# Second MLP, last block of 512 tokens: a seven-product contraction over two halves of 256 tokens, then the plain second contraction

## The chip, the cores and the metric

One NeuronCore of a Trainium2 chip runs the whole program in one launch. The metric is device time in microseconds (us). Engines are named as in the profile: PE (TensorE matmuls), PEld (TensorE weight loads, which overlap PE), DVE (VectorE), ACT (ScalarE), POOL (GpSimd) and SP (SyncE, which here only issues DMAs).

## What is computed

Attention without softmax and an RMS norm give 4608 tokens of 512 features. Two MLPs follow, each 512 -> 2048 -> 512, the first with a smooth clipped activation, the second with a squared ReLU. The change touches the second MLP alone:

```python
def _moe2_ref(x, w_in, w_out):       # x 4608 x 512, w_in 512 x 2048, w_out 2048 x 512
    h = x @ w_in
    r = np.maximum(h, 0.0)
    g = r * r
    return (g @ w_out).astype(np.float32)
```

All of it is asked for in float32. The kernel reaches that by splitting each operand into a high and a low part (type fp32r) and adding three matmuls for each product: high x high, high x low, low x high.

## The kernel before, in words

The 4608 tokens are handled as blocks of 512: eight blocks with the first 512 tokens of each batch, and a ninth (number 8) that collects the 64 remaining tokens of every batch. The first layer takes seven blocks one after the other (`h_stage`, `g_stage`, `out_stage`) while attention runs between them. After that, five steps each take two blocks at once, listed in `PAIRS` (line 130): (2,0), (2,2), (1, blocks 7 and 8), (2,4), (2,6), each entry the layer and its first block. Layer 2, block 8 is left, and is done at the end by plain contractions.

A step over two blocks uses a form of matrix multiplication with seven products of halves in place of eight. The halves are two of the tokens (the two blocks), two of the contracted dimension and two of the outputs. `in_phase(n)` (line 907) does the first contraction: 4 groups `q` of 7 `PRODUCTS` (order 1, 6, 2, 7, 5, 4, 3; line 70), for each product two output chunks `i`, and for each chunk two contracted chunks of three matmuls (`mm_group`, line 889), so 12 matmuls for one product. The seven products of a chunk gather in three PSUM banks (`bank_of`): the second product of a bank is added on top of what the first left there, after an engine has read it. ACT or DVE reads each bank after each product (lines 926 to 953) and makes the four quarters of the activated tile, `g2[k]`. `out_phase(n, jobs, at)` (line 964) does the second contraction in the same way, 56 steps, and its result stays in half of the `g2` tiles. During `out_phase(n)` the `jobs` prepare the tokens of the next step: `x2_jobs` (line 839) loads four chunks of the two blocks for each half of the features, and makes seven halved combinations `x2` of them.

The sums of halves of the weights were written to DRAM earlier (`wsd`). They come back as tiles of 512 KB, in exactly the order in which they are used (`w_order`, line 792). `take_w2` (line 816) hands over the next tile and issues, on SP, the load of the one seven places later; `w_ring` (line 783) has eight buffers, so that load waits until the matmuls on the tile before the present one are done.

The output of a step in layer 2 is written by four calls of `put_out` (line 1040). Each transposes two tiles on DVE and issues eight DMAs of 64 KB on SP, whose rows in DRAM are runs of 32 floats. The calls stand in the list `late` (line 1206) and are taken after products 0, 1, 5 and 9 of the next `in_phase` (line 1197), or after the first four steps of the last loop (line 1213). SP works through its queue in order: a weight load that stands behind eight of these DMAs is issued after them.

The last loop (lines 1208 to 1221) does block 8 of layer 2: 16 chunks `t` of the hidden dimension, each with 12 matmuls of the first contraction (`h_stage`, line 686, four feature chunks by three matmuls, 512 tokens wide), ACT and DVE for the activation and its two parts (`g_stage`, line 712), and, two steps behind (`LAG`), 12 matmuls of the second contraction with the activated tile as the stationary operand (`out_part`, line 718). One weight tile of each matrix is taken per chunk. `out_last` (line 746) finishes the last two chunks output by output and writes the results.

Of the kernel before, what the change touches and what calls it, by code (L numbers as in the profile page):

```python
# [9 lines left out]
F32 = mybir.dt.float32  # L10
# [66 lines left out]
def linear_attention_rms_two_mlps(  # L77
# [12 lines left out]
    nc = tc.nc  # L90
# [636 lines left out]
        mm3(acc[L, b][c], lhs, rhs, f == 0, f == NF - 1)  # L727

    def out_stage(L, b, f):
        if f == 0:  # L730
            acc[L, b] = [
                ps_a.tile([P, TB], F32, tag=f"acc{c}", name=f"acc{L}_{b}_{c}") for c in range(KD)
            ]
        for c in range(KD):
            out_part(L, b, f, c)
        del gs[L, b, f]
        if f == NF - 1:
            for c, a in enumerate(acc.pop((L, b))):
                t = st.tile([P, TB], F32, tag="st", name=f"ev{L}_{b}_{c}")
                if c % 2 == 0:  # L740
                    nc.vector.tensor_copy(t, a)
                else:
                    nc.scalar.copy(t, a)
                store(L, b, c, t)
# [48 lines left out]
    for L, _ in PAIRS:  # L793
        w_order += [(L, 0, q, p) for q in range(NQ) for p in PRODUCTS]
        w_order += [(L, 1, a, p) for p in PRODUCTS for a in range(NQ)]
    for f in range(NF + LAG):
        w_order += [(0, f)] * (f < NF) + [(1, f - LAG)] * (f >= LAG)
    w_loaded = []
    w_todo = iter(w_order)

# [15 lines left out]
    def take_w2(*key):  # L816


        found, t = w_loaded.pop(0)
        assert found == key, (found, key)  # L820
        load_w2()
        return t

    def halve(t, src, op):
        copy(engine2(op + "_hi"), t[:, 0, :], src)
        engine2(op + "_lo").tensor_tensor(t[:, 1, :], src, t[:, 0, :].bitcast(F32), ALU.subtract)  # L826

    x2 = {}

    def x_source(n, b, ch, t):  # L830

        L, b0 = PAIRS[n]
        if L == 2:
            return t, x1d[b0 + b][:, ch, :]
        if b == 0:
            return t, xpd[:, ch, :]
        return t.rearrange("p (b s) -> p b s", b=B), xrd[:, ch, :, :]

    def x2_jobs(n, ring):

        jobs = []
        for c in range(2):
            src = {}

            def load(c=c, src=src):
                for key, b, ch in ((11, 0, c), (12, 1, c), (22, 1, c + 2), (21, 0, c + 2)):
                    t = ring.tile([P, TB], F32, f"xr{n}_{c}_{key}")
                    nc.sync.dma_start(*x_source(n, b, ch, t))
                    src[key] = t

            def part(p, key, c=c, src=src, then=None):
                j = 7 * c + len([k for k in x2 if k[0] == n and k[2] == c])
                t = wp.tile([P, 2, TB], F32R, tag=f"w0_{j}", name=f"x2_{n}_{p}_{c}")
                halve(t, src[key], "x")
                x2[n, p, c] = t
                if then:
                    to, a, b = then
                    engine2("x_sum").tensor_tensor(src[to], src[a], src[b], ALU.subtract)  # L858

            jobs.append(load)  # L860

            for p, key, then in (
                (1, 11, (11, 12, 11)),
                (5, 11, (12, 22, 12)),
                (7, 12, (11, 22, 11)),
                (6, 11, None),
                (2, 21, (21, 21, 11)),
                (3, 22, None),
                (4, 21, None),
            ):  # L870
                jobs.append(lambda p=p, key=key, then=then, f=part: f(p, key, then=then))
        return jobs

    def x2_whole_jobs(L, b):
        src = {}

        def load(c):
            src[c] = tmp.tile([P, TB], F32, f"xr{b}_{c}")
            nc.sync.dma_start(src[c], x1d[b][:, c, :])

        def part(c):
            u = wp.tile([P, 2, TB], F32R, tag=f"w0_{c}", name=f"x2_{b}_{c}")
            halve(u, src[c], "x")
            xs.setdefault((L, b), []).append(u)

        order = ((load, 0), (load, 1), (part, 0), (load, 2), (part, 1), (load, 3), (part, 2), (part, 3))
        return [lambda f=f, c=c: f(c) for f, c in order]

    def mm_group(ps, lhs, rhs, first, last):

# [15 lines left out]

    def in_phase(n):

        for q in range(NQ):
            ps = {}  # L910
            e = {}
            for p in PRODUCTS:
                w = take_w2(PAIRS[n][0], 0, q, p)
                for i in range(2):
                    k = 2 * q + i
                    if p in FIRST:
                        ps[i, bank_of[p]] = ps_ring.tile([P, TB], F32, f"ph{n}_{p}_{k}")
                    bank = ps[i, bank_of[p]]
                    mm_group(
                        bank,  # L920
                        [lambda a, c=c: w[:, i, a, c * P : (c + 1) * P] for c in range(2)],
                        [lambda a, c=c: x2[n, p, c][:, a, :] for c in range(2)],
                        p in FIRST,
                        True,
                    )
                    if p == 1:
                        e[i, 1] = e_ring.tile([P, TB], F32, f"e1_{n}_{k}")
                        g2[k] = [
                            g_ring.tile([P, 2, TB], F32, f"g2_{n}_{k}_{j}") for j in range(2)
                        ]  # L930
                        nc.scalar.copy(e[i, 1], bank)
                    elif p in (6, 7):
                        kind = "e16" if p == 6 else "e167"
                        if p == 6:
                            e[i, 6] = e_ring.tile([P, TB], F32, f"{kind}_{n}_{k}")
                        else:
                            e[i, 7] = e_ring.tile([P, TB], F32, f"{kind}_{n}_{k}")
                        nc.vector.tensor_tensor(e[i, p], bank, e[i, 1], ALU.add)  # L938
                    else:
                        g = g2[k][0 if p in (2, 3) else 1][:, {2: 0, 3: 1, 4: 0, 5: 1}[p], :]  # L940
                        h = bank
                        if p != 2:
                            h = tmp.tile([P, TB], F32, f"h{n}_{p}_{k}")
                            add = e[i, {5: 7, 4: 1, 3: 6}[p]]
                            nc.vector.tensor_tensor(h, bank, add, ALU.add)  # L945
                        if PAIRS[n][0] == 1:
                            nc.scalar.activation(g, h, AF.Relu, bias=halfb, scale=0.5)
                            nc.scalar.activation(g, g, AF.Square)
                            nc.vector.scalar_tensor_tensor(g, g, 1.0, h, op0=ALU.min, op1=ALU.max)
                        else:  # L950
                            u = tmp.tile([P, TB], F32, f"u{n}_{p}_{k}") if p == 2 else h
                            nc.scalar.activation(u, h, AF.Relu)  # L952
                            nc.scalar.activation(g, u, AF.Square)  # L953
                yield
            for i in range(2):
                k = 2 * q + i
                a, b, d = g2[k][0][:, 0, :], g2[k][0][:, 1, :], g2[k][1][:, 1, :]
                t1[k] = t1_ring.tile([P, TB], F32, f"t1_{n}_{k}")
                engine2("t_sum").tensor_tensor(t1[k], b, a, ALU.subtract)
                engine2("t_sum").tensor_tensor(b, d, b, ALU.subtract)  # L960
# [227 lines left out]
        pay()  # L1188

    late = []  # L1190
    for n in range(NS):
        step_in = in_phase(n)
        for i, _ in enumerate(step_in):
            pay(True)
            if n == 0 and i < LAG:
                out_stage(*step(N1 - LAG + i))
            if late and i in (0, 1, 5, 9):
                late.pop(0)()
        while late:
            late.pop(0)()  # L1200
        result[n] = result_of(dict(g2))
        jobs = x2_jobs(n + 1, tmp) if n + 1 < NS else x2_whole_jobs(2, NB - 1)
        at = (2, *range(10, 8 + 2 * len(jobs), 2))
        for _ in out_phase(n, jobs, at):
            pass
        late = [lambda n=n, h=h: put_out(n, h // 2, h % 2) for h in range(4)]

    L, b = 2, NB - 1
    for t in range(NF + LAG):
        if t < NF:  # L1210
            wi[L, t] = take_w2(0, t)
            h_stage(L, b, t)
        if late:
            late.pop(0)()
        if t < NF:
            g_stage(L, b, t)
        if t >= LAG:
            wo[L, t - LAG] = take_w2(1, t - LAG)
        if LAG <= t < NF:
            out_stage(L, b, t - LAG)  # L1220
    out_last(L, b, *range(NF - LAG, NF))


# [34 lines left out]
```

## Time and profile before

| | us |
|---|---|
| median of 3 runs | 1565.77 (1565.66 to 1566.26) |
| the profiled execution: its own time | 1565.7 |
| its span, first to last instruction | 1563.9 |
| the two phases of the step before the last block | 1319.48 to 1395.64, and on to 1471.8 |
| last block, first to last matmul | 1471.8 to 1559.0 |

The page gives the busy time of each engine, the chain of work that ended last, and groups of instructions. A timeline lists instructions in order of time: when they began, how long the merged run of them lasted, engine, line, operation, what was written and read, shape and count; idle time of the engine just before stands in brackets with what ended it. The durations of single matmuls overlap each other, so the rate is read from the times at which runs begin. For a DMA the length is the time that SP spent on issuing it, and the landing is told apart.

### The profile page before, as it was taken

To read this page: it belongs to the slowest core of one execution; us is meant where nothing else is said; L and a number is where in the kernel's file an instruction comes from. 1 tells how busy PE (TensorE), PEld (TensorE's weight loads), DVE (VectorE), ACT (ScalarE), POOL (GpSimd) and SP (SyncE) were. 2 spreads that over 40 slices of the span, in tenths; PEclk is the share of its full clock that TensorE was granted. 3 is DMA by queue.
4 is the path that set the end of the run, shared out by engine and by line. 5 is a ranking of instruction groups with operands and counts; after the bars stand their busy time and mean duration, and the time that the engine had idled before them with its cause. 6 is when DMAs were issued, how large, how long until landed. Compare 5 with 4: busy or idle time off the path is not lost.

```text
span 1563.9 us, 21429 instructions
## 1 busy us (share of the span) xinstructions
PE 1553.6 (99%) x7437; PEld 1275.3 (82%) x7437; DVE 1097.4 (70%) x1871; ACT 940.1 (60%) x1719; POOL 17.3 (1%) x38
## 2 busy tenths in 40 slices
PE   9999999999999999999999999999999999999998
PEld 5788888888888888888888888888888888888887
DVE  6976786877877786754597559778956595667522
ACT  5977666767767676664664566466646663664321
POOL 0000000000000000000000000000000000000000
PEclk9999999999999999999999999999999999999999
DMA  9666899996987967835676867696776777876783
GB/s 289 198 210 184 280 325 274 315 316 176 272 257 238 281 204 239 282 96 174 190 247 197 235 206 246 194 248 205 246 229 199 228 214 198 242 220 192 189 252 108
DMA packets 327517, 355.59 MB, mean 227 GB/s; under 512 B 196465, under 2 KB 221041, under 8 KB 327409
## 3 DMA queue, kind: packets, MB, share of 16 engines
q1 hardware_dynamic: 295280, 295.76, 65.3%
q10 hardware_dynamic: 32128, 58.47, 10.0%
q8 instruction: 59, 0.97, 0.2%
q14 instruction: 50, 0.40, 0.1%
HBM read 270.01 MB, written 84.15 MB: 226 GB/s over the span
## 4 chain that ended last, share of the span: by engine, by line
PE 97%; ACT 1%; DVE 1%; DMA 1%; issue 0%; SPq 0%
PE po L893 24%; PE ph L893 24%; PE acc L237 23%; PE ph L237 21%; PE pkv L478 1%; PE po L237 1%; PE pr L600 1%; DMA raw<-in_moe_w_out_dram 1%; PE pwarm L1130 0%; PE po L568 0%; DMA v<-in_v_dram 0%; ACT raw L267 0%; PE pr L533 0%; DVE t L518 0%; PE po L510 0%; DVE t L522 0%
## 5 line engine op out<-in xcount | busy, mean ns | idle before, releaser
L893 PE MATMUL ph<-x,ws 128*128 128x512 f32 x1680 | 381.9, 389 | 0.0
L893 PE MATMUL po<-t,ws 128*128 128x512 f32 x1680 | 381.8, 389 | 0.0
L893 PEld LDWEIGHTS po<-t,ws 128*128 128x128 f32 x1680 | 315.3, 188 | 65.6 <-DVE t L826 0.3
L893 PEld LDWEIGHTS ph<-x,ws 128*128 128x128 f32 x1680 | 315.4, 188 | 65.4
L237 PE MATMUL ph<-x,w 128*128 128x512 f32 x1344 | 329.8, 392 | 2.4 <-ACT w L216 1.6
L237 PEld LDWEIGHTS ph<-x,w 128*128 128x128 f32 x1344 | 249.1, 188 | 55.8 <-ACT w L216 2.6
L826 DVE TENSOR_TENSOR t<-g,t 128x512 fp32r<-128x512 f32 x240 | 164.1, 688 | 85.4 <-ACT t L216 77.4
L216 ACT CAST t<-g 128x512 fp32r<-128x512 f32 x240 | 146.1, 621 | 87.6 <-DVE t L826 58.2
L237 PE MATMUL acc<-gs,w 128*128 128x512 f32 x696 | 173.7, 393 | 0.0
L237 PE MATMUL acc<-gs,wt 128*128 128x512 f32 x648 | 157.8, 391 | 0.0
L237 PEld LDWEIGHTS acc<-gs,w 128*128 128x128 f32 x696 | 129.1, 188 | 26.7 <-DVE u L706 0.3
L237 PEld LDWEIGHTS acc<-gs,wt 128*128 128x128 f32 x648 | 120.2, 188 | 24.3
L704 ACT ACTIVATE u<-ph,halfb 128x512 f32<-128x512 f32 x112 | 77.2, 690 | 103.6 <-PE ph L237 101.2
L945 DVE TENSOR_TENSOR h<-ph,e 128x512 f32<-128x512 f32 x120 | 82.5, 690 | 60.7 <-PE ph L893 54.2
L229 DVE TENSOR_TENSOR gs<-u,gs 128x512 fp32r<-128x512 f32 x128 | 88.1, 689 | 41.6 <-ACT gs L216 40.3
L706 DVE SCALAR_TENSOR_TENSOR u<-u,ph 128x512 f32<-128x512 f32 x112 | 76.3, 682 | 53.3 <-ACT u L223 52.8
L216 ACT CAST gs<-u 128x512 fp32r<-128x512 f32 x128 | 79.6, 622 | 49.8 <-DVE u L706 29.3
L952 ACT ACTIVATE h<-h 128x512 f32<-128x512 f32 x96 | 60.6, 631 | 56.2 <-DVE h L945 51.8
L938 DVE TENSOR_TENSOR e<-ph,e 128x512 f32<-128x512 f32 x80 | 54.6, 688 | 48.1 <-PE ph L893 47.1
L216 ACT CAST x<-xr 128x512 fp32r<-128x512 f32 x74 | 45.9, 621 | 42.9 <-DVE xr L858 19.5
L223 ACT ACTIVATE u<-u 128x512 f32<-128x512 f32 x112 | 70.7, 631 | 0.7
L953 ACT ACTIVATE g<-h 128x512 f32<-128x512 f32 x96 | 60.7, 632 | 2.6
(139 smaller groups left out, 1587.0 us busy)
## 6 DMA issues: line engine op xcount, KB each, us to landing
ws<-wsd SPq DMA_DIRECT2D x312, 512.0 KB, 4.3
wsd<-s ACTq DMA_DIRECT2D x96, 512.0 KB, 4.6
wt<-wsd SPq DMA_DIRECT2D x54, 512.0 KB, 5.1
raw<-in_moe_w_in_dram SPq DMA_DIRECT2D x32, 512.0 KB, 5.8
raw<-in_moe_w_out_dram SPq DMA_DIRECT2D x32, 512.0 KB, 6.0
xr<-x1d SPq DMA_DIRECT2D x36, 256.0 KB, 5.0
wsd<-w SPq DMA_DIRECT2D x17, 512.0 KB, 4.4
k<-in_k_dram SPq DMA_DIRECT2D x32, 256.0 KB, 5.6
```

Source lines behind the costliest of these rows:

```text
L216: return e.copy(dst, src)
L223: e.activation(dst, src, AF.Square)
L229: lo = engine(op + "_lo", phase).tensor_tensor(t[:, 1, :], src, t[:, 0, :].bitcast(F32), ALU.subtract)
L237: nc.tensor.matmul(dst, wt(a), xt(c), start=first and n == 0, stop=last and n == 2)
L704: nc.scalar.activation(u, ps, AF.Relu, bias=halfb, scale=0.5)
L706: nc.vector.scalar_tensor_tensor(u, u, 1.0, ps, op0=ALU.min, op1=ALU.max)
L826: engine2(op + "_lo").tensor_tensor(t[:, 1, :], src, t[:, 0, :].bitcast(F32), ALU.subtract)
L893: nc.tensor.matmul(ps, wt(a), xt(c), start=first and n == 0 and i == 0, stop=last and n == len(lhs) - 1 and i == 2, skip_group_check=True,)
L938: nc.vector.tensor_tensor(e[i, p], bank, e[i, 1], ALU.add)
L945: nc.vector.tensor_tensor(h, bank, add, ALU.add)
L952: nc.scalar.activation(u, h, AF.Relu)
L953: nc.scalar.activation(g, u, AF.Square)
```

## The change

The tokens of block 8 are given as two halves of 256 to the same seven-product form. `in_phase` runs a sixth time, `n = 5`, with a moving operand 256 wide and the layer-2 weight sums that the other layer-2 steps use; no `t1` sums are made, since no `out_phase` follows. The tiles keep their rings and buffers (PSUM banks, `e_ring`, `tmp`), of which the first 256 columns are used. The four quarters of `g2[k]` put side by side are then the 512 tokens of the chunks `k` and `k + 8`; the new `gates(f)` splits them into high and low parts, three chunks ahead (`LEAD`), and 16 `out_stage` steps follow, the last two in `out_last`, with unchanged matmuls. The accumulators now come from `ps_ring`. The weights of this block are 28 tiles of sums, then 16 plain tiles of the second matrix, where there were 16 and 16 in turn. `x2_whole_jobs` is gone; `x2_jobs` with `load_last` brings the same four 256 KB chunks and makes 14 halved tiles of 256 columns during `out_phase(4)`. The four `put_out` calls of the step before are now taken after products 0, 1, 5 and 9 of the new `in_phase(5)`.

```diff
-    for f in range(NF + LAG):
-        w_order += [(0, f)] * (f < NF) + [(1, f - LAG)] * (f >= LAG)
+    w_order += [(2, 0, q, p) for q in range(NQ) for p in PRODUCTS]
+    w_order += [(1, f) for f in range(NF)]
...
+            def load_last(c=c, src=src):
+                for keys, ch in (((11, 12), c), ((21, 22), c + 2)):
+                    t = tmp.tile([P, TB], F32, f"xr{n}_{ch}")
+                    nc.sync.dma_start(t, x1d[NB - 1][:, ch, :])
+                    for i, key in enumerate(keys):
+                        src[key] = t[:, i * H2 : (i + 1) * H2]
...
-                t = wp.tile([P, 2, TB], F32R, tag=f"w0_{j}", name=f"x2_{n}_{p}_{c}")
+                t = wp.tile([P, 2, width(n)], F32R, tag=f"w0_{j}", name=f"x2_{n}_{p}_{c}")
...
-    for n in range(NS):
+    for n in range(NS + 1):
         step_in = in_phase(n)
         for i, _ in enumerate(step_in):
             pay(True)
...
+        if n == NS:
+            break
         result[n] = result_of(dict(g2))
-        jobs = x2_jobs(n + 1, tmp) if n + 1 < NS else x2_whole_jobs(2, NB - 1)
+        jobs = x2_jobs(n + 1, tmp)
...
-    for t in range(NF + LAG):
-        if t < NF:
-            wi[L, t] = take_w2(0, t)
-            h_stage(L, b, t)
-        if late:
-            late.pop(0)()
-        if t < NF:
-            g_stage(L, b, t)
-        if t >= LAG:
-            wo[L, t - LAG] = take_w2(1, t - LAG)
-        if LAG <= t < NF:
-            out_stage(L, b, t - LAG)
+    def gates(f):
+        t = t_ring.tile([P, 2, TB], F32R, f"gs{L}_{b}_{f}")
+        halve(t, g2[f % NH][f // NH].rearrange("p a n -> p (a n)"), "t")
+        gs[L, b, f] = t
+        wo[L, f] = take_w2(1, f)
+
+    acc[L, b] = [ps_ring.tile([P, TB], F32, f"acc{L}_{b}_{c}") for c in range(KD)]
+    for f in range(NF):
+        for i in range(LEAD) if f == 0 else ():
+            gates(i)
+        if f + LEAD < NF:
+            gates(f + LEAD)
+        if f < NF - LAG:
+            out_stage(L, b, f)
     out_last(L, b, *range(NF - LAG, NF))
```

## Rows read from the trace of the kernel before

**Rows 1.** The page: busy time of PE and PEld, then the chain that ended last
```profile
PE 1553.6 (99%) x7437; PEld 1275.3 (82%) x7437; DVE 1097.4 (70%) x1871; ACT 940.1 (60%) x1719; POOL 17.3 (1%) x38
PE 97%; ACT 1%; DVE 1%; DMA 1%; issue 0%; SPq 0%
```
**Rows 2.** Windows: each engine's busy us and count, granted clock, DMA busy share, GB/s
```profile
1235.00:1312.00 77.00, 77.00 (x342) 63.75 (x340) 63.13 (x101) 46.89 (x80) 0.00 (x0) 1.00 0.72 221
1471.00:1564.00 93.00, 88.00 (x389) 72.53 (x387) 27.77 (x41) 20.47 (x34) 0.00 (x0) 0.99 0.66 180
```
**Rows 3.** Groups by shape: busy us, mean ns of one; 288 columns and their weight loads
```profile
L237 PE MATMUL ph<-x,ws 128*128 128x512 f32 x192 | 45.8, 389 | 0.0
L237 PEld LDWEIGHTS po<-qT,kvbd 128*128 128x128 f32 x144 | 24.8, 188 | 4.8 <-DVE qT L559 0.4 <-ACT qT L216 0.4
```
**Rows 4.** Timeline of PE: attention's matmuls of 288 columns between others of 512
```profile
684.18 0.55 PE L237 MATMUL po<-qT,kvbd 128*128 128x288 f32 x3
684.57 2.90 PE L237 MATMUL acc<-gs,wt 128*128 128x512 f32 x12
687.30 0.57 PE L237 MATMUL po<-qT,kvbd 128*128 128x288 f32 x3
```
**Rows 5.** Timeline of PE: the start of the first contraction of step 4
```profile
1319.48 4.70 PE L893 MATMUL ph<-x,ws 128*128 128x512 f32 x20
```
**Rows 6.** Timeline of SP in step 4's first contraction: weight loads (ws), output DMAs (ov)
```profile
1319.67 0.32 SPq L809 DMA_DIRECT2D ws<-wsd  x1
1320.33 3.69 SPq L1063 DMA_DIRECT2D out_dram<-ov  x6
1324.11 0.44 SPq L809 DMA_DIRECT2D ws<-wsd  x1
1324.64 5.09 SPq L1063 DMA_DIRECT2D out_dram<-ov  x8
1329.84 3.75 SPq L809 DMA_DIRECT2D ws<-wsd  x4
1333.68 5.52 SPq L1063 DMA_DIRECT2D out_dram<-ov  x8
1339.30 5.17 SPq L809 DMA_DIRECT2D ws<-wsd  x4
1344.52 5.54 SPq L1063 DMA_DIRECT2D out_dram<-ov  x8
1350.16 0.92 SPq L809 DMA_DIRECT2D ws<-wsd  x2
```
**Rows 7.** SP's waits, 1319.4 to 1351 us: line, releaser, us in total, times, longest
```profile
SPq L809 <- PE ph L893: 6.1, 6, 2.3
```
**Rows 8.** Weight loads issued back to back in the last block: issue ns, issue times, landing
```profile
L813 SPq DMA_DIRECT2D ws<-wsd x6: 420/427/475, 1496.6 to 1499.3; - x6
...
DMA to landing us min/median/max: 4.0/6.0/7.9
```
**Rows 9.** Windows (columns as in rows 2): output DMAs with loads; loads nearly alone
```profile
1324.10:1350.10 26.00, 26.00 (x117) 21.52 (x116) 15.00 (x23) 14.78 (x25) 0.00 (x0) 1.00 0.94 243
1500.00:1506.00 6.00, 6.00 (x28) 4.97 (x27) 1.93 (x3) 1.22 (x2) 0.00 (x0) 1.00 1.04 396
```
**Rows 10.** DMA issues: engine, count, KB each, median us from issue to landing
```profile
ws<-wsd SPq DMA_DIRECT2D x312, 512.0 KB, 4.3
```
**Rows 11.** Groups by shape: ACT on 288 columns, DVE on 256
```profile
L581 ACT ACTIVATE wk<-po 128x288 f32<-128x288 f32 x48 | 19.8, 412 | 0.0
L364 DVE TENSOR_TENSOR s<-d,s 128x256 f32<-128x256 f32 x16 | 6.7, 420 | 0.2
```
**Rows 12.** Timeline of ACT and PE: a cast, and the second contraction's start
```profile
1367.08 0.60 ACT L216 CAST t<-g 128x512 fp32r<-128x512 f32 x1
...
1395.64 10.59 PE L893 MATMUL po<-t,ws 128*128 128x512 f32 x46
```
**Rows 13.** Windows (columns as in rows 2), 2 us after PE's last matmul
```profile
1561.00:1562.00 1.00, 0.00 (x0) 0.00 (x0) 0.00 (x0) 0.00 (x0) 0.00 (x0) 0.68 0.92 258
```

More of the change, by code (lines that the diff above doesn't have):

```diff
@@ L729, in out_stage @@
     def out_stage(L, b, f):
-        if f == 0:
+        if (L, b) not in acc:
             acc[L, b] = [
@@ L828, in linear_attention_rms_two_mlps, with width, layer @@
     x2 = {}
+    def width(n):
+        return TB if n < NS else H2
+    def layer(n):
+        return PAIRS[n][0] if n < NS else 2
     def x_source(n, b, ch, t):
@@ L858, in part @@
                     engine2("x_sum").tensor_tensor(src[to], src[a], src[b], ALU.subtract)
-            jobs.append(load)
+            jobs.append(load if n < NS else load_last)
             for p, key, then in (
@@ L872, in x2_jobs @@
         return jobs
[L874 to L887, printed above, removed]
     def mm_group(ps, lhs, rhs, first, last):
@@ L907, in in_phase, with tile @@
     def in_phase(n):
+        N = width(n)
+        def tile(ring, name):
+            return ring.tile([P, TB], F32, name)[:, :N]
         for q in range(NQ):
@@ L912, in in_phase @@
             for p in PRODUCTS:
-                w = take_w2(PAIRS[n][0], 0, q, p)
+                w = take_w2(layer(n), 0, q, p)
                 for i in range(2):
@@ L916, in in_phase @@
                     if p in FIRST:
-                        ps[i, bank_of[p]] = ps_ring.tile([P, TB], F32, f"ph{n}_{p}_{k}")
+                        ps[i, bank_of[p]] = tile(ps_ring, f"ph{n}_{p}_{k}")
                     bank = ps[i, bank_of[p]]
@@ L926, in in_phase @@
                     if p == 1:
-                        e[i, 1] = e_ring.tile([P, TB], F32, f"e1_{n}_{k}")
+                        e[i, 1] = tile(e_ring, f"e1_{n}_{k}")
                         g2[k] = [
-                            g_ring.tile([P, 2, TB], F32, f"g2_{n}_{k}_{j}") for j in range(2)
+                            g_ring.tile([P, 2, N], F32, f"g2_{n}_{k}_{j}") for j in range(2)
                         ]
@@ L934, in in_phase @@
                         if p == 6:
-                            e[i, 6] = e_ring.tile([P, TB], F32, f"{kind}_{n}_{k}")
+                            e[i, 6] = tile(e_ring, f"{kind}_{n}_{k}")
                         else:
-                            e[i, 7] = e_ring.tile([P, TB], F32, f"{kind}_{n}_{k}")
+                            e[i, 7] = tile(e_ring, f"{kind}_{n}_{k}")
                         nc.vector.tensor_tensor(e[i, p], bank, e[i, 1], ALU.add)
@@ L942, in in_phase @@
                         if p != 2:
-                            h = tmp.tile([P, TB], F32, f"h{n}_{p}_{k}")
+                            h = tile(tmp, f"h{n}_{p}_{k}")
                             add = e[i, {5: 7, 4: 1, 3: 6}[p]]
                             nc.vector.tensor_tensor(h, bank, add, ALU.add)
-                        if PAIRS[n][0] == 1:
+                        if layer(n) == 1:
                             nc.scalar.activation(g, h, AF.Relu, bias=halfb, scale=0.5)
@@ L950, in in_phase @@
                         else:
-                            u = tmp.tile([P, TB], F32, f"u{n}_{p}_{k}") if p == 2 else h
+                            u = tile(tmp, f"u{n}_{p}_{k}") if p == 2 else h
                             nc.scalar.activation(u, h, AF.Relu)
@@ L954, in in_phase @@
                 yield
-            for i in range(2):
+            for i in range(2 if n < NS else 0):
                 k = 2 * q + i
```

## The prediction

> **What bounds the kernel now.** I read the page first: PE is busy for 99% of the span and carries 97% of the chain of work that ended last [rows 1]. Then the windows by stage: the last stretch, 1471 to 1564, has PE busy until its final matmul, with DVE and ACT at a quarter of the time, the clock at its full level of 2.4 GHz and the DMA engines two thirds busy [rows 2]. So only matmul time, or something that makes PE wait, moves the end. A busy PE says nothing of its rate: the groups show 389 ns for a matmul, which overlaps the next one [rows 3]. The timeline gives the rate: 12 matmuls of 512 columns from 684.57 to 687.30, 227 ns each; three of 288 columns from 684.18 to 684.57, 130 ns each [rows 4]. Last I read SP's queue in step 4, where four `put_out` calls stand among weight loads just as they will in the new `in_phase(5)` [rows 5 to 10].
>
> **Removed and added on PE.** The first contraction of block 8 was 16 chunks x 12 = 192 matmuls of 512 columns: 192 x 0.227 = 43.6 us. It becomes 28 products x 12 = 336 matmuls of 256 columns. No row has 256 columns. The line through 130 ns at 288 and 227 ns at 512 gives 116 ns (a rounding of 0.01 us in rows 4 is 3 ns); 130 is the other end, since fewer columns should not take longer unless the weight load is the limit. I take 120, nearer to the line: 336 x 0.120 = 40.3 us, so -3.3 us (ends: -4.6 and +0.1). A product then lasts 12 x 0.120 = 1.44 us, where one of step 4 lasts 12 x 0.227 = 2.72. One eighth of the multiplications goes, but a matmul of half the width costs more than half. The second contraction keeps its 192 matmuls of 512 columns.
>
> The weight loads show 188 ns each, in the group of 288 columns too, while those matmuls follow each other every 130 ns [rows 3, 4]; so 188 ns is no spacing there. The Trainium skill (Perfetto Trace Analysis, section Identifying the Most-Contended Engine) has it that headroom on TensorE is judged by the busy share of the weight loads, not by that of the matmuls. Read strictly, 82% in rows 1 would leave less than a fifth; this case's trace disagrees for runs of three to six matmuls, and it has no long run, so the rule stands as a rival below.
>
> **The weight tiles, where the new wait comes from.** Call T the start of `in_phase(5)` and tile j the weights of product j. Tiles 0 to 6 are there, tile 7 is issued at T, and without waits tile j is due at T + 1.44 j. In step 4 T is 1319.48 [rows 5], and SP's order is: tile 7, the last six DMAs of the first `put_out`, tile 8, eight DMAs, tiles 9 to 12, eight, tiles 13 to 16, eight, tile 17 and the rest [rows 6]. This follows from the place of the calls (after products 0, 1, 5 and 9), which the change keeps, so I take the same order. At 2.72 us per product nothing of it delayed PE. At 1.44 the lead of seven tiles shrinks from 19 to 10 us, while the output DMAs cost the same.
> - Tile 9: SP comes to it at 1329.84, T + 10.4 [rows 6]. Nothing before it depends on the pace of the products but tile 8's buffer, which is free earlier. A load right behind eight output DMAs landed after 4.0 us [rows 8], so it is there at T + 14.4 and due at 13.0: PE waits 1.4 us.
> - Tile 17, by SP alone: its issue in step 4 is at 1350.16, T + 30.7 [rows 6]. The two groups of four loads before it took 3.75 and 5.17 us because SP waited there for PE to free buffers (6.1 us in all in that stretch, rows 7); unhindered loads follow every 0.54 us [rows 8], so four take 2.0, and at the faster pace (3.75 - 2.0) + (5.17 - 2.0) = 4.9 us go. That leaves T + 25.8, and landing at 29.8.
> - Tile 17, by the DMA engines: one load is 0.524 MB, at 396 GB/s 1.32 us [rows 9]; six loads issued together landed after 4.0 to 7.9, which agrees (the last landing less the first, over five) [rows 8]. Between 1324.1 and 1350.1 the engines were 0.94 busy, 24.4 us, and moved 26.0 x 243 GB/s = 6.32 MB: 24 output DMAs of 0.066 MB, and the rest about 9 loads, 12 us. So an output DMA costs 12.4 / 24 = 0.52 us of the engines. From T to tile 17 they have 11 loads and 30 output DMAs: 14.5 + 15.6 = 30.1 us, and 2.9 for start and landing (a lone load takes 4.3, rows 10, of which 1.32 is moving): T + 33.
>
> Tile 17 is due at 24.5, so the waits up to it sum to 5.3 (SP alone) or 8.5 us (engines). I take 32, so 7.5: the engines were already 0.94 busy while SP stood still for 4.9 us, so they are the nearer limit. The wait falls in three places, before products 9, 13 and 17, each behind a `put_out`: about 1.5, 3 and 3 us. After that loads come every 1.32 us and a product takes 1.44, then a second-contraction tile every 2.72, so nothing more is lost.
>
> **Parts that cost nothing here.** ACT gets 9 operations of 256 columns for each of 8 chunks (one copy, four times ReLU and square). Between 0.412 us for 288 columns and less [rows 11], 72 x 0.41 = 29.5 us of some 47; per group of seven products 7.4 of 10.1 us. DVE: 40 additions x 0.42 [rows 11] = 17 us and eight transposes. The tightest link is the copy of product 1, which must leave its bank before product 2 adds to it, 2.2 us later: a copy of 0.4 fits, if ACT is not still busy with the group before. I take 0, with up to +1.5 if that cover fails (three group borders of 0.5). The start of the second contraction: chunks 0 to 5 need only the first three groups, and in step 4 such casts were made 28 us ahead and PE went on without idle time [rows 12]; chunk 6 is due 16 us later. 0. The jobs in `out_phase(4)`: the same four loads, 10 more halvings of half the width and 6 subtractions, some 5 us more of DVE; the like stretch of step 3 had the full 512-wide set, DVE 63 of 77 us, and PE unbroken [rows 2]. 0. The tail is unchanged.
>
> **Sum.** Against the profiled execution, 1565.7 us (span 1563.9, and 1.8 around it; the median of the runs is 0.1 higher): -3.3 + 7.5 = +4.2, so 1570. The case's own range: waits of 5.3 to 8.5 us with -3.3, and 130 ns or a slow link of ACT on top: 1567.5 to 1573.
>
> **Rivals.**
> - Loads keep up. If SP's order puts the weight loads ahead of the output DMAs, tile 9 is issued near T + 5 instead of 10.4, and the engines have 21 loads, 28 us, before the last product at T + 39, with the outputs left for the second contraction. Then only PE counts: 1565.7 - 3.3 = 1562.4, up to 1567 if only part is hidden. Against it stands the order in rows 6. Its decisive point is where tile 9 stands against the second `put_out`.
> - The clock falls in a wait. About 2 us after the last matmul the granted clock is on its way down, 0.68 in that microsecond [rows 13]. My second and third wait are about 3 us long. At 1.2 GHz a product takes twice 1.44; a few products so after the third wait, which nothing hides, cost about 2 to 4 us: 1572 to 1575.
> - The evictions of the halved tiles pace PE: ACT at a group border, +1.5 us after the waits: 1571.5 or a little above.
> - Weight loads are the limit: at 188 ns spacing 336 x 0.188 = 63.2 us, 19.6 above the old 43.6, and a product of 2.26 us is slow enough for the tiles: 1585. That is where the skill's rule would lead.
>
> **How the numbers follow.** Forecast as said 0.62; loads keep up 0.13; the clock 0.11; evictions 0.08; weight loads 0.04; anything else 0.02. The bound of what can be told from no change is 0.2%, 3.1 us: 1562.6 and 1568.9. Of the forecast's own 1567.5 to 1573 about three tenths lie below 1568.9, and of the case in which loads keep up half lies below 1562.6. Faster 0.07, same 0.26, slower 0.67. The range reaches from part of the case where loads keep up to the clock's: 1564.5 to 1575.
>
> **What would show it.** A 256-column matmul every 120 ns in the first contraction; three waits of PE there, of 1 to 4 us, just before products 9, 13 and 17, released by DMAs on `ws`; SP's order as in rows 6, with tile 17 issued about 26 to 29 us after T; no idle time at the change to the second contraction; the whole block some 91 us from first to last matmul, where it was 87. I am wrong if PE runs through without idle time (then 1562), if the spacing is near 188 ns, or if the waits are released by ACT or DVE.

## The result, and the profile after

| | before | after |
|---|---|---|
| median, us | 1565.9 | 1576.3 (1573.6 to 1578.4) |
| ratio to before, 95% interval | | 1.0065 [1.0054, 1.0075] |
| profiled execution: its own time, span | 1565.7, 1563.9 | 1575.9, 1574.2 |
| last block's first matmul | 1471.8 | 1472.6 |
| its last matmul's end | 1559.0 | 1569.7 |

The change costs 10.4 us. It was forecast slower, by 4.2, and the time lies above the range.

Here is the timeline of PE after, from the end of step 4's second contraction (`po`) over the new first contraction (`ph`, 336 matmuls of 256 columns) to the second (`acc`). Brackets give PE's idle time just before, and what ended it.

```profile
1464.68 8.10 PE L891 MATMUL po<-t,ws 128*128 128x512 f32 x35
1472.61 13.11 PE L891 MATMUL ph<-x,ws 128*128 128x256 f32 x108
1488.93 7.49 PE L891 MATMUL ph<-x,ws 128*128 128x256 f32 x48 [3.20 <-DMA ws<-wsd]
1498.54 7.48 PE L891 MATMUL ph<-x,ws 128*128 128x256 f32 x48 [2.12 <-DMA ws<-wsd]
1508.64 17.55 PE L891 MATMUL ph<-x,ws 128*128 128x256 f32 x132 [2.62 <-DMA ws<-wsd]
1526.03 4.27 PE L237 MATMUL acc<-ws,gs 128*128 128x512 f32 x18
```

Divide the counts by 12: PE runs through products 0 to 8, waits for a weight tile, does four, waits, does four, waits, and does the last eleven. These are the places that were forecast, before products 9, 13 and 17. The change to the second contraction has no idle time. With T = 1472.61, the start of the first contraction, product 17 begins at T + 36.0, where it would be due at T + 24.5: it is 11.5 us late. The brackets add up to 7.9. Nearly all of the other 3.6 lies in products 9 to 16, two groups of four that lasted 7.5 us each, where four at 1.44 are 5.8; the clock, below, was low there.

The timeline of SP in the same stretch, which answers to [rows 6]:

```profile
1472.81 0.32 SPq L809 DMA_DIRECT2D ws<-wsd  x1
1473.18 4.24 SPq L1066 DMA_DIRECT2D out_dram<-ov  x6
1477.52 2.00 SPq L809 DMA_DIRECT2D ws<-wsd  x1
1479.62 5.18 SPq L1066 DMA_DIRECT2D out_dram<-ov  x8
1484.89 1.88 SPq L809 DMA_DIRECT2D ws<-wsd  x4
1486.86 7.45 SPq L1066 DMA_DIRECT2D out_dram<-ov  x8
1494.41 1.87 SPq L809 DMA_DIRECT2D ws<-wsd  x4
1496.33 8.10 SPq L1066 DMA_DIRECT2D out_dram<-ov  x8
1504.52 10.50 SPq L809 DMA_DIRECT2D ws<-wsd  x11
```

The order is that of step 4. The groups of four loads no longer wait for PE (1.9 us each, where they took 3.75 and 5.17). But the eight output DMAs behind four loads take 7.45 and 8.10 us, where [rows 6] had 5.52 and 5.54, and tile 8 (the third line) took 2.00 to issue in place of 0.44. In all the stretch from tile 9 to tile 17 SP waited for PE for 0.8 us. Tiles 9, 13 and 17 are the first loads of the last three groups; each landed 3.9 to 4.0 us after its issue, and PE went on then.

Windows (columns as in rows 2): the stretch from T to product 17; the first wait and the 2 us after it; then three stretches from product 17 on.

```profile
1472.60:1508.60 36.00, 28.09 (x205) 27.53 (x203) 14.37 (x31) 17.47 (x46) 0.00 (x0) 0.91 0.90 234
...
1486.00:1489.00 3.00, 0.07 (x1) 0.10 (x1) 1.21 (x3) 0.00 (x0) 0.00 (x0) 1.00 0.95 285
1489.00:1491.00 2.00, 2.00 (x12) 2.00 (x13) 0.00 (x0) 0.80 (x2) 0.00 (x0) 0.66 1.05 406
1508.60:1512.50 3.90, 3.86 (x23) 3.90 (x24) 1.27 (x3) 0.36 (x1) 0.00 (x0) 0.69 1.02 416
1512.50:1516.00 3.50, 3.50 (x27) 3.50 (x27) 1.70 (x4) 2.79 (x9) 0.00 (x0) 0.85 1.04 425
1516.00:1526.00 10.00, 10.00 (x85) 10.00 (x85) 4.75 (x11) 6.75 (x20) 0.00 (x0) 1.00 1.03 408
```

The granted clock (1.00 is 2.4 GHz) was still full in the first wait. It fell when PE was at work again, to the lower level of 1.2 GHz for part of the time: 0.66 in the mean of the 2 us after the first wait, 0.69 and 0.85 after the third. So the last eleven products took 1526.03 - 1508.64 = 17.4 us, where 11 x 1.44 are 15.9.

### The profile page after: what moved, and what is told of

Read it like the earlier page. It is cut to its first block, busy times and chain, and to the rows that moved or that the text cites. A ratio compares the mean times of both kernels' runs of the same rounds, so it can differ in the third digit from the quotient of the medians.

```text
span 1574.2 us, 21880 instructions
## 1 busy us (share of the span) xinstructions
PE 1555.8 (99%) x7581; PEld 1284.3 (82%) x7581; DVE 1106.9 (70%) x1913; ACT 958.9 (61%) x1785; POOL 18.9 (1%) x38
## 4 chain that ended last, share of the span: by engine, by line
PE 96%; DMA 1%; DVE 1%; ACT 1%; SPq 1%; issue 0%; DVEq 0%
PE ph L891 26%; PE po L891 24%; PE acc L237 22%; PE ph L237 18%; PE pkv L478 1%; PE po L237 1%; PE pr L600 1%; DMA ws<-wsd 1%; SPq L1066 0%; DMA raw<-in_moe_w_out_dram 0%; DMA v<-in_v_dram 0%; PE pwarm L1133 0%; PE po L568 0%; ACT raw L267 0%; PE pr L533 0%
## 5 line engine op out<-in xcount | busy, mean ns | idle before, releaser
L891 PE MATMUL ph<-x,ws 128*128 128x512 f32 (+1 forms) x2016 | 427.6, 375 | 7.9 <-DMA ws<-wsd 7.9
L891 PEld LDWEIGHTS ph<-x,ws 128*128 128x128 f32 x2016 | 360.5, 192 | 73.9 <-issue 8.5
L948 DVE TENSOR_TENSOR h<-ph,e 128x512 f32<-128x512 f32 (+1 forms) x144 | 92.7, 646 | 72.0 <-PE ph L891 64.5
L955 ACT ACTIVATE h<-h 128x512 f32<-128x512 f32 (+1 forms) x120 | 70.3, 586 | 70.3 <-DVE h L948 65.8
L941 DVE TENSOR_TENSOR e<-ph,e 128x512 f32<-128x512 f32 (+1 forms) x96 | 61.1, 644 | 63.4 <-PE ph L891 62.4
L229 DVE TENSOR_TENSOR gs<-u,gs 128x512 fp32r<-128x512 f32 x112 | 77.1, 688 | 24.4 <-ACT gs L216 23.8
L216 ACT CAST gs<-u 128x512 fp32r<-128x512 f32 x112 | 69.6, 622 | 33.0 <-DVE u L706 29.5
L956 ACT ACTIVATE g<-h 128x512 f32<-128x512 f32 (+1 forms) x120 | 70.7, 589 | 3.2
L216 ACT CAST x<-xr 128x512 fp32r<-128x512 f32 (+1 forms) x84 | 48.9, 586 | 38.8 <-DVE xr L871 17.7
```

The costliest lines, as they stand in the source:

```text
L216: return e.copy(dst, src)
L229: lo = engine(op + "_lo", phase).tensor_tensor(t[:, 1, :], src, t[:, 0, :].bitcast(F32), ALU.subtract)
L891: nc.tensor.matmul(ps, wt(a), xt(c), start=first and n == 0 and i == 0, stop=last and n == len(lhs) - 1 and i == 2, skip_group_check=True,)
```

## The experiments

The theory: weight tiles stand behind the output DMAs of step 4 in SP's queue. The rivals: the loads alone are too much; the DMA engines' total work is too much in any order; the price lies in the short runs of the output DMAs; the clock.

**The output DMAs left out (e1), and left out of the kernel before (b1).** In `put_out`, for step 4 alone:

```diff
-                nc.sync.dma_start(rows[a], src)
+                if n != NS - 1:
+                    nc.sync.dma_start(rows[a], src)
```

> Leaves out the 32 output DMAs of step 4 (their transposes stay), so two blocks of the output are never written. Theory (weight tiles queue behind the output DMAs): no wait of PE on ws, clock at its full level, 3.3 us below the kernel before, 1562.6. Rival (the weight loads alone, a tile every 1.44 us, are too much for the DMA engines): waits on ws remain, 1566 or more.

> The kernel before without the 32 output DMAs of step 4 (two blocks of the output are never written). Theory: at 2.72 us per tile pair of 12 matmuls they cost nothing, 1565.9. Rival (they slow something in the kernel before as well, so that e1 gained more than the waits): 1563 or less.

Measured: e1 1562.5 (1561.8 to 1563.0), ratio 0.9977 [0.9968, 0.9986]; b1 1565.6, ratio 0.9997 [0.9987, 1.0006]. PE's timeline in e1:

```profile
1472.07 40.48 PE L891 MATMUL ph<-x,ws 128*128 128x256 f32 x336
1512.38 43.71 PE L237 MATMUL acc<-ws,gs 128*128 128x512 f32 x192
```

All three waits are gone, and the 336 matmuls take 1512.38 - 1472.07 = 40.31 us, 120 ns each, the value taken in the sum. So the same DMAs that cost the kernel before nothing cost the changed one some 14 us, and the loads alone can keep up.

**The output DMAs spread among the loads (e4).** The step's output is transposed into the eight `t1_ring` buffers, of which the last block uses seven, and only for its results at the very end, and the 32 DMAs are sent one or two at a time. `send(k)` issues the next `k` of them on SP:

```diff
+            ts = [t1_ring.tile([P, TB], F32, f"ov{n}_{hn}_{hm}_{m}") for m in range(2)]
...
+                    outs.append((rows[a], src))
...
             if late and i in (0, 1, 5, 9):
                 late.pop(0)()
+            if n == NS:
+                send(1 + (i % 7 == 6))
```

> As e2, but the 32 output DMAs are issued one after each product of the first contraction (two after each seventh). If only the bunches of eight hurt (SP has 0.54 + 0.66 us to issue per product of 1.44): no wait, 1562.6. If the sum of the engines' work decides (1.32 + 0.54 to 0.62 us per product of 1.44): PE is late by about 4 us at the last products, 1566 to 1568. If neither order nor place matters: 1576.

Measured: 1562.4 (1561.5 to 1563.2), ratio 0.9977 [0.9968, 0.9986], with the whole output written. SP's timeline in e4:

```profile
1471.48 13.27 SPq L809 DMA_DIRECT2D ws<-wsd  x10
1484.80 0.43 SPq L1205 DMA_DIRECT2D out_dram<-ov  x1
1485.87 0.32 SPq L809 DMA_DIRECT2D ws<-wsd  x1
...
1516.17 1.50 SPq L1205 DMA_DIRECT2D out_dram<-ov  x2
1517.77 16.16 SPq L813 DMA_DIRECT2D ws<-wsd  x9
```

Three output DMAs went out before T. From T on SP issued ten loads first, although a call stands after each product, then one output DMA (now and then two) after each load, until 1517.7, some 6 us into the second contraction. PE ran through: its 336 matmuls took 1471.28 to 1511.60. A window of that stretch has the DMA engines full, with a share of 1.02:

```profile
1471.30:1511.60 40.30, 40.30 (x338) 40.30 (x337) 21.96 (x49) 26.86 (x73) 0.00 (x0) 1.00 1.02 332
```

So it is the order that decides. The engines' sum of work, which in one case of the expectation makes PE late by some 4 us, does not: what is late are output DMAs, and nobody waits for them. Whether the ten loads in front or the single output DMAs behind them did it, this run does not tell.

**Long runs (e3).** The same 32 DMAs in the same places write 32 rows of 2 KB each:

```diff
+                if n == NS - 1:
+                    r0 = b * S + ((2 * hm + m) * MR + a) * 32
+                    rows = {a: out[r0 : r0 + 32, :]}
+                    src = t[a * 32 : (a + 1) * 32, m, :]
```

> Same 32 output DMAs of 64 KB at the same places, but each writes 32 rows of 2 KB in place of 512 runs of 128 bytes, so the two blocks are written in another arrangement. If the engines' time for short runs (0.54 us per DMA) is the cost: tile 17 lands at T + 30 or sooner, waits of 5 us at most in place of 11.5, 1563 to 1569. If the number of DMAs on SP and its stalls are the cost: unchanged, 1574 to 1577.

Measured: 1570.1 (1568.5 to 1570.9), a little over the upper end of the first case. PE's timeline, SP's, and the window from T to product 17:

```profile
1471.91 18.91 PE L891 MATMUL ph<-x,ws 128*128 128x256 f32 x156
1493.54 7.48 PE L891 MATMUL ph<-x,ws 128*128 128x256 f32 x48 [2.72 <-DMA ws<-wsd]
1502.61 16.07 PE L891 MATMUL ph<-x,ws 128*128 128x256 f32 x132 [1.59 <-DMA ws<-wsd]
```

```profile
1475.35 4.73 SPq L1070 DMA_DIRECT2D out_dram<-ov  x8
1480.92 1.77 SPq L809 DMA_DIRECT2D ws<-wsd  x4
1482.78 6.57 SPq L1070 DMA_DIRECT2D out_dram<-ov  x8
1489.44 1.83 SPq L809 DMA_DIRECT2D ws<-wsd  x4
1491.32 6.73 SPq L1070 DMA_DIRECT2D out_dram<-ov  x8
1498.15 9.36 SPq L809 DMA_DIRECT2D ws<-wsd  x11
```

```profile
1471.90:1502.60 30.70, 26.40 (x205) 26.03 (x204) 14.09 (x31) 17.49 (x46) 0.00 (x0) 0.94 0.84 273
```

The wait before product 9 is gone and product 17 begins at 1502.61, T + 30.7 in place of T + 36.0. So about 5 of the 11.5 us are the price of the short runs, and 6 remain with runs sixteen times as long. (This execution is the fastest of e3's, 1.6 us below their median, so the 5 may be somewhat less.) The groups show what remains: eight DMAs take 4.7 us behind one load and 6.6 to 6.7 behind four, though they cost the engines less. An estimate from this window and that of the trace after (the engines' busy time, less the other bytes at the 396 GB/s of [rows 9], over 30 DMAs) is 0.32 us of the engines for a DMA with long runs and 0.54 for one with short runs.

**The clock (e5), beside the changed kernel run again (a1).** Matmuls that nobody reads stand before products 9, 13 and 17:

```diff
+                if n == NS and (q, p) in ((1, 2), (1, 3), (2, 7)):
+                    idle = tile(ps_ring, f"idle_{q}_{p}")
+                    for _ in range(24):
+                        nc.tensor.matmul(
+                            idle, w[:, 1, 0, P:], x2[n, 1, 0][:, 0, :], start=True, stop=True
+                        )
                 w = take_w2(layer(n), 0, q, p)
```

> The changed kernel unchanged, on this chip, for comparison with the next run: 1576, three waits on ws, tile 17 at T + 36, clock below its full level after each wait.

> The changed kernel with 24 matmuls of 256 columns more before each of products 9, 13 and 17, on data that is there, into a bank nobody reads: they fill 2.9 us of each wait. If the clock falls because PE stands still and this costs time after the last wait: granted clock 1.0 throughout, the last 11 products in 15.9 in place of 17.4 us, 1574.5. If the low clock costs nothing that the next wait doesn't hide: 1576. If the waits are not what they seem and these matmuls are simply more work: 1580 and above.

Measured: a1 1577.5 (1575.5 to 1577.7), e5 1574.7 (1573.3 to 1576.7), ratios to before 1.0070 [1.0056, 1.0083] and 1.0056 [1.0043, 1.0068]. PE's timeline in a1:

```profile
1472.21 13.32 PE L891 MATMUL ph<-x,ws 128*128 128x256 f32 x108
1489.46 8.10 PE L891 MATMUL ph<-x,ws 128*128 128x256 f32 x48 [3.93 <-DMA ws<-wsd]
1498.99 5.98 PE L891 MATMUL ph<-x,ws 128*128 128x256 f32 x48 [1.42 <-DMA ws<-wsd]
1509.57 18.34 PE L891 MATMUL ph<-x,ws 128*128 128x256 f32 x132 [4.61 <-DMA ws<-wsd]
1527.75 43.71 PE L237 MATMUL acc<-ws,gs 128*128 128x512 f32 x192
```

My expectation for a1 was off in two points: product 17 began at T + 37.4, not 36, and after the second wait, of 1.42 us, the clock was not low (four products in 5.98 us). PE's timeline and the window of the first contraction in e5:

```profile
1485.06 3.04 PE L919 MATMUL idle<-x,ws 128*128 128x256 f32 x24
1487.94 5.92 PE L891 MATMUL ph<-x,ws 128*128 128x256 f32 x48
1493.70 3.04 PE L919 MATMUL idle<-x,ws 128*128 128x256 f32 x24
1498.43 6.04 PE L891 MATMUL ph<-x,ws 128*128 128x256 f32 x48 [1.70 <-DMA ws<-wsd]
1504.31 3.04 PE L919 MATMUL idle<-x,ws 128*128 128x256 f32 x24
1508.08 16.30 PE L891 MATMUL ph<-x,ws 128*128 128x256 f32 x132 [0.73 <-DMA ws<-wsd]
1524.22 43.71 PE L237 MATMUL acc<-ws,gs 128*128 128x512 f32 x192
```

```profile
1472.00:1525.00 53.00, 50.57 (x414) 49.88 (x413) 22.43 (x50) 27.84 (x75) 0.00 (x0) 1.00 0.94 291
```

The clock stayed at 1.0 in the profiled execution. Product 17 still began at T + 36.0 (1508.08 less 1472.11), as in the trace after, so the low clock was not what held the tiles back. (Between that trace and a1 it differs by 1.4 us, so an effect smaller than that can't be told.) The last eleven products took 16.1 us, against 17.4 after and 18.2 in a1. The clock so costs 1.3 to 2.1 us after the last wait. The two intervals of the whole time overlap, so the size rests on the traces and not on the medians.

**The output DMAs moved into the second contraction (e2, e7, e9).** As e4, but `send(2 + f % 2)` after each `out_stage` (e2), `send(4)` (e7), and e7 with all final writes issued by SP (e9):

```diff
-            e = nc.scalar if c == 1 or (c == KD - 1 and j == 1) else nc.sync
-            e.dma_start(out[r0 : r0 + REM, :], t[j * REM : (j + 1) * REM, :])
+            nc.sync.dma_start(out[r0 : r0 + REM, :], t[j * REM : (j + 1) * REM, :])
```

> Transposes of step 4's output go to eight other buffers at the same places; the 32 output DMAs are issued in the second contraction, two or three per chunk. Theory: no wait on ws in the first contraction and enough slack in the second (a tile per 2.72 us), 1562.6, below both kernels. Rival (the outputs only carry their cost along): waits of PE in the second contraction or a later end, 1566 or more.

> As e2, but four output DMAs per chunk of the second contraction, so that all are issued by its eighth chunk. If e2 lost its 4 us only because its last two output DMAs and the final writes stood behind a DMA of ACT's at the very end: 1562.5. If output DMAs in the second contraction cost time wherever they stand: 1566.

> As e7, but the three final writes that ACT issues are issued by SP too. In e2 and e7 SP stood 11 to 13 us before its last two output DMAs until a final write of ACT's had landed, and its own final writes were late by that. If this wait is the 4 us: it is gone, the end comes near e1's plus the issuing of three more writes on SP (0.9 us each), 1563 to 1565. If the output DMAs in the second contraction are late by themselves: 1566.5 as before.

Measured: e2 1566.8, ratio 1.0004 [0.9995, 1.0012]; e7 1566.5, 1.0002 [0.9993, 1.0011]; e9 1563.0, 0.9978 [0.9969, 0.9988]. My expectation for e2 was wrong, and so was the cure in e7. PE's timelines are those of e1: in e7 the two contractions begin at 1472.85 and 1513.16 with no idle time. The 4 us are at the very end. SP's waits in e7, its timeline there, and that in e9:

```profile
SPq L1205 <- DMA out_dram<-ev: 13.2, 2, 12.9
```

```profile
1537.57 20.49 SPq L1205 DMA_DIRECT2D out_dram<-ov  x12
1558.16 4.37 SPq L761 DMA_DIRECT2D out_dram<-ev  x5
```

```profile
1537.18 7.08 SPq L1204 DMA_DIRECT2D out_dram<-ov  x12
1552.85 5.32 SPq L760 DMA_DIRECT2D out_dram<-ev  x8
```

SP had two output DMAs left and stood 12.9 us until a final write that ACT had issued was done; its own final writes came behind that, at 1558.2. Sending earlier in e7 did not take those two away from there. With every final write on SP (e9) the wait is gone, the last twelve output DMAs take 7.1 us in place of 20.5, and 3.5 us are back.

## Why the prediction was wrong, by its own steps

- **What bounds the kernel, matmul time, weight loads:** right. 120 ns per matmul of 256 columns (e1), -3.3 us. The rival in which weight loads of 188 ns are the limit is out: in the new first contraction they show 192 ns at the median while matmuls follow every 120. The Trainium skill (Perfetto Trace Analysis, section Identifying the Most-Contended Engine) judges TensorE's headroom by the time of the weight loads over the window, and by MFU, the useful arithmetic over the peak, which the prediction left out. The trace disagrees with the first as a limit, in a run of 336 too: 336 loads of 192 ns are 64.5 us, and in e4 they lie within 40.3 us (PEld busy 40.30 of 40.30), so the loads shown overlap each other.
- **Parts that cost nothing:** right. ACT and DVE show no wait of PE, the second contraction begins at once, and the jobs in `out_phase(4)` are hidden.
- **The mechanism of the waits:** right in order, place and releaser, and e1, b1 and e4 show it: the output DMAs, their order on SP, and the faster pace of the products together.
- **The size of the wait up to tile 17, the step that failed:** taken as 7.5 between 5.3 and 8.5, measured 11.5. I had made two separate estimates, SP alone (T + 29.8) and the engines alone (T + 33), and put the value between them. The larger of two limits that work on one queue is a floor, not an upper end, and here both were too low. That PE's idle time adds up to 7.9, near 7.5, is chance: products 9 to 16, slow at the low clock, took up most of the rest of the 11.5.
  - SP alone took it that the 4.9 us in which SP stood for PE in step 4 would simply go. Only 0.7 went. Four loads and the eight output DMAs behind them took SP 9.27 and 10.71 us in [rows 6], its waits for PE included, and 9.33 and 9.97 in the trace after, almost without such waits: the loads were issued 5.2 us sooner, and the output DMAs behind them took 4.5 us longer. By the prediction's own prices such a group is 9.4 us of work for the engines (4 x 1.32 + 8 x 0.52). My reading is that they had worked off the four loads while SP stood, and that without the wait SP ran into that backlog. The sum is 25.8 + 1.6 (tile 8) + 1.9 + 2.6 (the two groups behind four loads) = T + 31.9 for the issue of tile 17, as measured, and 4 to land.
  - The engines' estimate had 30.1 us of work and 2.9 for start and landing. Measured over the 36.0 us: 0.90 busy, so 32.4 of work, and 3.6 idle. They moved 36.0 x 234 GB/s = 8.42 MB, where 11 loads and 30 output DMAs are 7.73; the rest, some 1.7 us at 396 GB/s, belongs more likely than not to later tiles, which is not shown apart.
  - e3 splits the 11.5 another way: some 5 us for the short runs, and 6 that stay with long ones.
- **The clock:** put as a rival at 0.11, of 2 to 4 us. It was no alternative to the forecast but part of it, since it follows from the waits: 1.5 us in this trace. Sum by the steps: -3.3 + 11.5 + 1.5 = 9.7; the rest of 10.2 is the earlier part of the execution (the last block began 0.8 later, of which some 0.6 stand already at the first matmuls of the program) less a tail 0.4 shorter.
- **The rival in which loads keep up:** e4 makes it come true at its decisive point, with tile 9 issued ahead of nearly all output DMAs, and gives 1562.4, the time that was worked out for it. That took another kernel; in the changed kernel as it stood the order was the forecast one.

What stays open: why tile 8 took 2.00 us to issue in the profiled execution (0.43 in a1, where instead the six DMAs before it took 6.08), and why a group behind four loads takes 2 us longer than one behind a single load even with long runs. The profile puts 1.8 of the 2.00 us down to PE, but the matmuls on tile 0, whose buffer tile 8 takes, were done more than 3 us before. A queue of DMAs in flight that is full is my reading, from one DMA in each of the two groups behind four loads that took 2.6 and 2.2 us to issue, where the median is 0.5 to 0.6; it was not tested apart.

## What to carry to other kernels

A stage that is made faster takes its buffered lead with it: seven tiles were 19 us of lead at 2.72 us per product and 10 at 1.44, and a queue in which eight slow DMAs stood before a load went from free to 11 us. Look at what else is issued on the loads' queue in bunches, and put it behind the loads, one by one, or where nobody waits; here that turned +10.4 into -3.7 us. And where two limits share a queue, take the larger one as the least that it will cost.

## What the runs showed of the hardware that was not expected

- Once PE waits on a bunch of DMAs, their variation is in the time: the changed kernel spreads over 4.8 us (1573.6 to 1578.4), the one before, in the same set, over 0.6. In its two profiled executions product 17 began at T + 36.0 and T + 37.4. How SP's time splits varies in step 4 too, where no one waits for it: in [rows 6] four loads took 3.75 us and the group behind them 5.52, together 9.3, and in the trace after 2.27 and 7.33, together 9.6:

```profile
1332.14 2.27 SPq L809 DMA_DIRECT2D ws<-wsd  x4
1334.50 7.33 SPq L1066 DMA_DIRECT2D out_dram<-ov  x8
```

- In the trace after, the granted clock was 1.00 in the first wait, of 3.2 us, and 0.66 in the 2 us that followed, with PE at work. In a1, whose first wait was 3.9 us, it was already 0.78 in the mean of 1485.0 to 1489.4, which is that wait and little else. After idle times of 2.1 to 3.9 us four products took 7.5 to 8.1 us (after, e3, a1); after 1.4 and 1.7 us they took 6.0 (a1, e5).
- Issuing a DMA on SP can wait for the landing of one that another engine issued, 12.9 us here (e7), and that wait went with the other engine's DMAs (e9). Whether the chip or the program's own order asks for it is not shown.
